# Dealing the half tiles of K and V to the partitions in another order, in a two-layer decode kernel on one core

## The chip, the cores and the metric

The kernel runs on one core of a Trainium2 chip, and the other cores are idle. The metric is the time of one execution on the device, in microseconds (us). The kernel before has three runs, 320.61, 322.80 and 325.11 us; the median is 322.8 us.

## What is computed

One decode step (a single new position) for a batch of four goes through attention, feed-forward, attention and feed-forward again, with the same weights and the same cache both times. Cut to what matters:

```python
B, Sq, D, Hq, Hkv, Sk, Dh, F = 4, 1, 512, 32, 8, 4096, 128, 1792   # all bfloat16

def attention(x):                     # 4 query heads share a K/V head
    q = (x @ wq) by heads
    p = softmax(q @ k_cache.T * Dh ** -0.5)      # over 4096 keys
    return (p @ v_cache) by heads @ wo

def feed_forward(x):
    return (sigmoid(x @ w_gate) * (x @ w_up)) @ w_down

for layer in range(2):
    x = x + attention(layernorm(x))
    x = x + feed_forward(layernorm(x))
```

The K cache and the V cache hold 4 x 8 x 4096 x 128 bfloat16 each, 33.5 MB each. A softmax and the sum over values that follows do not depend on the order of the keys, as long as K and V are in the same order.

## The kernel before

**Units and half tiles.** A unit is one batch row b, one group hg of four K/V heads and one layer l: 4 x 2 x 2 = 16 units, in the order of the list `seq` (L483). A unit has four streams s (one K/V head each), and each stream's 4096 keys are loaded as two half tiles, q = 0 and 1, of K and two of V. A half tile is [128 partitions x 2048 elements], 16 keys of 128 elements in each partition, 512 KB in all. In the kernel before, partition p owns the 32 keys from 32p on: 8 KB of the source. Half tile q takes the 4 KB of them that hold the keys 32p + 16q to 32p + 16q + 15 (L514). So a half tile's source is 128 rows of 4 KB, 8 KB apart, spread over the 1 MB of its stream.

**The ring and the queue.** Half tiles go to a ring of 23 slots (`SLOTS`, L371; `ring`, L384). Every load of K, V and weights is issued by SyncE (SP), one after the other, in the order in which `load_kv` (L509), `load_w` (L520) and the lists of L559 to L581 write them down. Before a load into a slot that was used, SP waits for the instructions that read the slot's last content. Layer 2 reads the cache again. Only the units with hg = 1 of layer 2 find their half tiles still in the ring (`kept`, L492): those of (b, 1, 0) stay in 16 of the slots until (b, 1, 1) has used them, and meanwhile seven slots turn. That makes 96 half tiles of K and 96 of V that are loaded.

**The planner.** The class `_Plan` (L68) takes each operation with a cost, a rank and the names that it reads and writes, plays the program through with an own model of the engines and the DMA (`DMA_RATE` L13, `schedule` L127), and fixes the order on each engine, the slots, and the semaphore waits. A load has size 0.524 and cost 0.5 there (L516). During idle time of TensorE the planner puts filler matmuls (L1119) that compute nothing that is used.

**What happens to a half tile.** A K half tile is transposed in place by VectorE in 32x32 blocks of 4-byte words (L747), then TensorE multiplies it with the queries (L756) into the scores. Scores of both half tiles of a stream are summed into one bank per unit, each half using its own shifted window of the query tile (`window`, L734), so that the probabilities of q = 0 and q = 1 stay in separate rows. The maximum, the exponential and the transposes of the probabilities follow (L778 to L813). A V half tile is multiplied as it lies by the transposed probabilities (L838). After that come the copy out of the bank (L849), the sums over partitions (L854, L861) and the output projection (L870).

**Feed-forward.** For each batch row, `chain` (L984) computes the norm, gate and up products (L932), the gated product (L952 to L964), the down product (L974) and the norm again, from which the queries of layer 2 are made. The last one, for all four rows together, is `last_chain` (L1032) after the last values.

The weights come through the same queue: wq as two loads of 2 MB, wo as four of 1 MB, wg, wu and wd as one load each of 1.75 MB.

Of the kernel before, what the change touches and what calls it, by code (L numbers as in the profile page):

```python
# [348 lines left out]
def bass_interleave_layers__gqa_block_cached__glu_gated_glu__decode_kernel(nc, A_x, A_k, A_v, A_wq, A_wo, B_x, B_wg, B_wu, B_wd, out):  # L349
# [5 lines left out]
    P = 128  # L355
# [4 lines left out]
    NS = 4  # L360
# [4 lines left out]
    TH = T // 2  # L365
# [130 lines left out]
    def tile(kind, b, hg, l, s, q):  # L496
        if l == 1 and hg == 1 and (s, q) in kept[kind]:
            l = 0
        key = (kind, b, hg, l, s, q)
        if key not in tiles:  # L500
            tiles[key] = _Tile(key)
        return tiles[key]

    def fresh(kind, hg, l, s, q):
        return not (l == 1 and hg == 1 and (s, q) in kept[kind])
# [3 lines left out]
    def load_kv(kind, u, s, q):  # L509
        b, hg, l = u  # L510
        if not fresh(kind, hg, l, s, q):
            return
        t = tile(kind, b, hg, l, s, q)
        src = (A_k if kind == "k" else A_v)[b, hg * NS + s].rearrange("(p t) d -> p t d", p=P)[:, q * TH:(q + 1) * TH, :]  # L514
        src = src.rearrange("p t d -> p (t d)")
        S.put("sp", lambda e: e.dma_start(ring[t.slot], src), dma="ring", load=t, size=0.524, cost=0.5)  # L516
        sent[0] += 0.524 / DMA_RATE
        place[kind, u, s, q] = sent[0]
# [25 lines left out]
    def mixed(uk, uv, by):  # L544
        k, v = k_order(uk), v_order(uv)
        for n in range(0, len(k), by):
            for t in k[n:n + by] + v[n:n + by]:
                load_kv(*t)

    def alone(order):  # L550
        for t in order:
            load_kv(*t)
# [607 lines left out]
```

## Time and profile before

| what | value |
| --- | --- |
| runs | 320.61, 322.80, 325.11 us |
| profiled execution: own time | 324.57 us |
| profiled execution: span | 322.9 us |
| mean granted TensorE clock | 0.873 |
| read from HBM | 114.56 MB, 355 GB/s over the span |
| DMA packets | 34931 |
| half tiles of K: issues, median from issue to landing | 96, 9.6 us |
| half tiles of V: issues, median from issue to landing | 96, 14.3 us |
| transposes of K on VectorE (L747) | 96, 1230 ns each, 116.9 us |

The span goes from the first to the last instruction of the profiled execution. Busy times are given as a share of that span. The page also cuts the span into 40 slices of 8.07 us; a digit there is the busy share in tenths, and "GB/s" is what the 16 DMA engines moved in the slice. In the chain that ended last, "DMA" stands for time in which a transfer was on its way, "SPq" for SP's queue.

### The profile page before, as it was taken

How to read it: one execution, taken by the hardware profiler on the slowest of the kernel's cores; microseconds unless marked ns; L12 is line 12 of the kernel's file. 1: busy time of each engine (PE TensorE's matmuls, PEld its weight loads, DVE VectorE, ACT ScalarE, POOL GpSimd, SP SyncE). 2: the span in 40 equal slices, each digit the busy share in tenths (PEclk: the TensorE clock that was granted, in tenths of full speed). 3: DMA queues.
4: the chain of work that ended last, by engine and by line, in shares of the span. 5: the costliest groups of instructions: out<-in, count | busy, mean ns of one | idle time of the engine just before them, and what ended most of it. 6: DMA issues, size and time to landing. Idle time of an engine off the chain costs nothing.

```text
span 322.9 us, 7748 instructions
## 1 busy us (share of the span) xinstructions
PE 216.9 (67%) x3401; PEld 115.8 (36%) x3401; DVE 169.6 (53%) x314; ACT 60.6 (19%) x151; POOL 12.6 (4%) x44
## 2 busy tenths in 40 slices
PE   1243455486869864878774797686896776758685
PEld 1213114333436431335522346233444332324343
DVE  3677250582011889215978326787327777537112
ACT  0202010003102311122131232050322322200301
POOL 8000000000000000000000000000000000000001
PEclk9999995969785987689979999878998999586978
DMA  7999999999999999999799999899998799999910
GB/s 266 402 411 409 401 376 352 404 410 409 396 406 354 306 414 411 407 394 317 229 338 410 410 409 336 287 399 370 412 390 338 202 407 410 409 406 410 393 45 3
DMA packets 34931, 115.09 MB, mean 356 GB/s; under 512 B 3280, under 2 KB 7376, under 8 KB 34896
## 3 DMA queue, kind: packets, MB, share of 16 engines
q1 hardware_dynamic: 34832, 114.57, 93.5%
q8 instruction: 27, 0.44, 0.6%
q14 instruction: 8, 0.07, 0.0%
q10 hardware_dynamic: 64, 0.01, 0.0%
HBM read 114.56 MB, written 0.00 MB: 355 GB/s over the span
## 4 chain that ended last, share of the span: by engine, by line
DMA 54%; PE 21%; SPq 9%; DVE 9%; issue 3%; ACT 2%; POOL 0%; DVEq 0%; ACTq 0%
DMA ring<-in_A_v_cache_dram 24%; DMA ring<-in_A_k_cache_dram 18%; SPq L516 7%; DMA wd<-in_B_w_down_dram 7%; DMA wo<-in_A_wo_dram 6%; DVE ring L747 5%; PE O_ps L838 5%; PE S_ps L756 4%; PE G_ps L974 2%; PE PT_ps L1119 2%; PE M_ps L870 2%; SPq L521 2%; PE Q_ps L676 1%; PE G_ps L932 1%; PE U_ps L932 1%
## 5 line engine op out<-in xcount | busy, mean ns | idle before, releaser
L747 DVE STREAM_TRANSPOSE ring<-ring 128x1024 int32<-128x1024 int32 x96 | 116.9, 1230 | 32.3 <-DMA ring<-in_A_k_cache_dram 31.1
L756 PE MATMUL S_ps<-ring,qz 128*32 128x512 bf16 x512 | 46.0, 485 | 28.6 <-DVE ring L747 26.7
L838 PE MATMUL O_ps<-ring,pt_sb 128*16 128x512 bf16 x512 | 45.8, 443 | 23.5 <-DMA ring<-in_A_v_cache_dram 21.9
L1119 PE MATMUL PT_ps<-even 128*128 128x256 bf16 x311 | 55.1, 317 | 8.1 <-ACT pt_sb L813 3.4
L1119 PEld LDWEIGHTS PT_ps<-even 128*128 128x128 bf16 x311 | 30.9, 114 | 28.3 <-issue 9.9
L849 ACT ACTIVATE b<-O_ps 128x512 bf16<-128x512 f32 x32 | 19.0, 595 | 81.0 <-PE O_ps L838 80.9
L756 PEld LDWEIGHTS S_ps<-ring,qz 128*32 128x32 bf16 x512 | 13.5, 110 | 48.7 <-DVE ring L747 30.5
L792 ACT ACTIVATE pp<-S_ps,tr 128x512 bf16<-128x512 f32 x16 | 13.3, 832 | 73.8 <-DVE tr L785 70.0
L838 PEld LDWEIGHTS O_ps<-ring,pt_sb 128*16 128x16 bf16 x512 | 9.8, 90 | 40.8 <-issue 21.7
L778 DVE TENSOR_REDUCE stat<-S_ps 128x1 f32<-128x512 f32 x16 | 10.9, 684 | 23.1 <-PE S_ps L756 23.1
L861 DVE TENSOR_TENSOR oT<-M_ps,rl 128x8 bf16<-128x8 f32 x32 | 4.8, 149 | 32.4 <-PE M_ps L854 32.3
L870 PE MATMUL M_ps<-oT,wo 128*128 128x32 bf16 x512 | 16.1, 180 | 5.7 <-DMA wo<-in_A_wo_dram 3.4
L870 PEld LDWEIGHTS M_ps<-oT,wo 128*128 128x128 bf16 x512 | 14.4, 98 | 9.6 <-issue 5.4
L854 PE MATMUL M_ps<-sel_o,b 128*128 128x32 bf16 x128 | 8.5, 181 | 9.2 <-ACT b L849 7.0
L922 POOL TENSOR_TENSOR stat<-stat 128x1 f32<-128x1 f32 x8 | 4.3, 543 | 232.1 <-ACT stat L918 232.1
L854 PEld LDWEIGHTS M_ps<-sel_o,b 128*128 128x128 bf16 x128 | 5.5, 98 | 20.1 <-ACT b L849 16.7
L813 ACT ACTIVATE pt_sb<-PT_ps 128x512 bf16<-128x512 f32 x16 | 9.5, 596 | 15.5 <-PE PT_ps L803 15.5
L817 PE MATMUL M_ps<-sel_h,stat 128*128 128x16 f32 x32 | 6.7, 285 | 6.9 <-ACT pp L792 6.6
L882 DVE SCALAR_TENSOR_TENSOR x<-M_ps,x 128x4 f32<-128x4 f32 x16 | 2.5, 156 | 16.0 <-PE M_ps L870 16.0
L974 PE MATMUL G_ps<-pp,wd 128*128 128x32 bf16 x256 | 7.4, 179 | 4.7 <-DVE pp L964 4.7
L798 DVE STREAM_TRANSPOSE pp<-pp 128x256 int32<-128x256 int32 x16 | 6.9, 431 | 6.0 <-ACT pp L792 6.0
L676 PE MATMUL Q_ps<-small,wq 128*128 128x32 bf16 x256 | 8.1, 179 | 2.4 <-issue 2.2
(112 smaller groups left out, 161.6 us busy)
## 6 DMA issues: line engine op xcount, KB each, us to landing
ring<-in_A_k_cache_dram SPq DMA_DIRECT2D x96, 512.0 KB, 9.6
ring<-in_A_v_cache_dram SPq DMA_DIRECT2D x96, 512.0 KB, 14.3
wq<-in_A_wq_dram SPq DMA_DIRECT2D x2, 2048.0 KB, 13.9
wo<-in_A_wo_dram SPq DMA_DIRECT2D x4, 1024.0 KB, 15.1
wg<-in_B_w_gate_dram SPq DMA_DIRECT2D x1, 1792.0 KB, 16.2
wu<-in_B_w_up_dram SPq DMA_DIRECT2D x1, 1792.0 KB, 20.3
wd<-in_B_w_down_dram SPq DMA_DIRECT2D x1, 1792.0 KB, 22.2
xin<-in_A_x_dram ACTq DMA_DIRECT2D x1, 4.0 KB, 3.4
```

The source lines that it names most:

```text
L516: S.put("sp", lambda e: e.dma_start(ring[t.slot], src), dma="ring", load=t, size=0.524, cost=0.5)
L676: fns.append(lambda e, c=c, k=k: e.matmul(Q_ps[:, c * WIDE:(c + 1) * WIDE], lhsT=wq[:, hg, k, c * DH:(c + 1) * DH], rhs=xT[:, b, k:k + 1]. ...
L747: "dve", lambda e, t=t: e.transpose(ring[t.slot].bitcast(dt.int32), ring[t.slot].bitcast(dt.int32)),
L756: fns.append(lambda e, s=s, t=t, nn=nn, q=q: e.matmul(S_ps[qi][32 * s:32 * s + 32, :], lhsT=window(qi, s * NQ + nn, q), rhs=ring[t.slot].r ...
L778: dve(lambda e: e.tensor_reduce(ml[at], bank, AX.X, ALU.max, negate=True), keys(f"S{qi}", ss), keys("ml", ss), 0.7)
L792: lambda e: e.activation(p_sb[at].rearrange("p (t j r) -> p t r j", j=32, r=2), bank.rearrange("p (t r j) -> p t r j", r=2, j=32), ACTF.Ex ...
L838: fns.append(lambda e, m=m, at=at, v=v, c=c, q=q: e.matmul(O_ps[m:m + 16, :], lhsT=pt[:, at:at + 16], rhs=ring[v.slot][:, c * 512:(c + 1) ...
L849: "act", lambda e: e.activation(b1[:], O_ps[:], ACTF.Copy),
L854: fns.append(lambda e, tt=tt: e.matmul(M_ps[:, 0:WIDE], lhsT=b1[:, tt * P:(tt + 1) * P], rhs=sel_o[:, tt, :].unsqueeze(1).broadcast_to([P, ...
L870: fns.append(lambda e, k=k, n=n, h0=h0: e.matmul(M_ps[:, k * WIDE:(k + 1) * WIDE], lhsT=wo[:, h0 + n, k * P:(k + 1) * P], rhs=oT[:, b, h0 ...
L974: fns.append(lambda e, k=k, c=c, rows=rows: e.matmul(o_ps[:, k * WIDE:(k + 1) * WIDE], lhsT=wd[:, c, k * P:(k + 1) * P], rhs=rows.unsqueez ...
L1119: S.filler(lambda e: e.matmul(PT_ps[:, 0:256], lhsT=ident, rhs=flat_even[:, 0:256], start=True, stop=True), "PT")
```

## The change

One source pattern changes, that of the half tiles of K and V. Before, half q of a stream was the q-th 4 KB of every partition's 8 KB. After, half q is the q-th straight 512 KB of the stream, 2048 neighbouring keys. It is seen as 128 runs of 4 KB (16 keys); run number 16i + e, with i from 0 to 7 and e from 0 to 15, goes to partition 8e + i. Two neighbouring runs of the source are thus eight partitions apart. The source pattern has the levels e (16), i (8) and the 4 KB; the destination is the same slot with 128 partitions.

```diff
         t = tile(kind, b, hg, l, s, q)
-        src = (A_k if kind == "k" else A_v)[b, hg * NS + s].rearrange("(p t) d -> p t d", p=P)[:, q * TH:(q + 1) * TH, :]
-        src = src.rearrange("p t d -> p (t d)")
+        src = (A_k if kind == "k" else A_v)[b, hg * NS + s, q * TH * P:(q + 1) * TH * P].rearrange("(i e t) d -> e i (t d)", i=8, e=16)
         S.put("sp", lambda e: e.dma_start(ring[t.slot], src), dma="ring", load=t, size=0.524, cost=0.5)
```

K and V are dealt in the same way, so the key in a given partition and place of a K half tile is the key in that place of the V half tile. Nothing else in the program differs.

## The prediction

> **What bounds the kernel now.** First the page's busy shares and its 40 slices.
>
> ```profile
> PE 216.9 (67%) x3401; PEld 115.8 (36%) x3401; DVE 169.6 (53%) x314; ACT 60.6 (19%) x151; POOL 12.6 (4%) x44
> ...
> DMA  7999999999999999999799999899998799999910
> GB/s 266 402 411 409 401 376 352 404 410 409 396 406 354 306 414 411 407 394 317 229 338 410 410 409 336 287 399 370 412 390 338 202 407 410 409 406 410 393 45 3
> ```
>
> No engine is full, but the transfers are, from the start to slice 37. Many slices stand at 406 to 414 GB/s and none goes beyond: that is a ceiling. Others lie at 200 to 350 although the busy digit stays at 8 or 9. The list of queues and the chain of waits say the same: nearly everything is one queue, and the chain is mostly half tiles on their way.
>
> ```profile
> q1 hardware_dynamic: 34832, 114.57, 93.5%
> ...
> DMA 54%; PE 21%; SPq 9%; DVE 9%; issue 3%; ACT 2%; POOL 0%; DVEq 0%; ACTq 0%
> DMA ring<-in_A_v_cache_dram 24%; DMA ring<-in_A_k_cache_dram 18%; SPq L516 7%; DMA wd<-in_B_w_down_dram 7%; DMA wo<-in_A_wo_dram 6%; DVE ring L747 5%; PE O_ps L838 5%; PE S_ps L756 4%; PE G_ps L974 2%; PE PT_ps L1119 2%; PE M_ps L870 2%; SPq L521 2%; PE Q_ps L676 1%; PE G_ps L932 1%; PE U_ps L932 1%
> ```
>
> Third, stretches by window. The columns are start and end, length, busy time of PE, PEld, DVE, ACT and POOL, the granted clock, DMA share and GB/s.
>
> ```profile
> 161.50:165.00 3.50, 2.32 (x33) 1.00 (x35) 2.55 (x4) 1.27 (x4) 0.00 (x0) 0.66 0.88 247
> 166.00:176.00 10.00, 6.30 (x90) 2.89 (x82) 9.40 (x15) 2.35 (x5) 0.00 (x0) 1.00 1.03 411
> 253.50:257.50 4.00, 3.08 (x54) 1.57 (x58) 3.77 (x6) 1.74 (x5) 0.00 (x0) 1.00 0.84 235
> 260.00:270.00 10.00, 7.82 (x170) 3.86 (x158) 6.71 (x15) 2.76 (x7) 0.00 (x0) 1.00 1.02 412
> 47.00:53.00 6.00, 2.62 (x62) 1.74 (x62) 1.03 (x4) 1.76 (x4) 0.00 (x0) 0.75 1.10 348
> 75.00:80.00 5.00, 3.41 (x75) 1.73 (x63) 0.33 (x2) 1.09 (x2) 0.00 (x0) 1.00 1.03 409
> ```
>
> The reader is to see two states of the same stream. In the even state (166 to 176, 260 to 270) 512 KB come at 411 GB/s: 1.28 us for each half tile. Just after the stream had run dry (161.5 to 165, 253.5 to 257.5) the engines are 84 to 88% busy and move only 235 to 247. The trace's packet records give the mechanism: in the even state a 4 KB packet takes 159 ns at the median, and its eight packets and one 4-byte packet of 9 ns per engine make 8 x 159 + 9 = 1281 ns, the 1.28 us again. After a break the same packets take anything from 159 to some 400 ns for two or three half tiles, and then all fall back to 159. No half tile is missing then, since SP issues one every half microsecond; the engines get in each other's way until they have fallen into step. The half tiles issued at 158.4, 158.7 and 159.4 have their first landing increments at 161.26, 163.30 and 165.29: 2.02 us each. The last two windows are straight weights: 1 KB packets of wo at 348 GB/s, mostly 3.5 KB packets of wg and wu at 409.
>
> Fourth, why the stream runs dry: SP's own waits.
>
> ```profile
> SPq L516 <- PE O_ps L838: 39.6, 16, 8.6
> ...
> SPq L516 <- PE S_ps L756: 22.4, 9, 7.8
> ```
>
> SP waits for readers to give back a slot of the ring. Most of these waits lie under half tiles that are already queued; the rest are the breaks at slices 12, 13, 18, 19, 24, 25, 30 and 31.
>
> **The budget.** The last landing is at 309.45 us. Bytes begin to flow at 2.9 (the first wq lands at 8.0, less 5.1 for its 2 MB). The weights need, by their landings, 2 x 5.1 (wq), 4 x 3.0 (wo), 4.5, 4.5 and 4.65 (wg, wu, wd): 35.9. 192 half tiles x 1.28 are 245.8. That leaves 309.45 - 2.9 - 35.9 - 245.8 = 24.9. Adding up every landing that comes later than its size asks for gives 22.9; the other 2 are the spread of the last half tile over the engines (3.5 us from its first increment to its last). Of the 22.9, 11.8 fall where the half tile had long been issued and others were queued (the slow restarts), 11.1 where it had been issued too late (no free slot). After 309.45 come 13.4 us of last values, projection and feed-forward. Span 322.9; this execution's own time is 324.57, 1.7 more, and the median of the three runs is 322.8, 1.8 less.
>
> **The change part by part.** Removed: a source of 128 rows of 4 KB with a step of 8 KB over 1 MB. Added: a source of 16 x 8 runs of 4 KB in one straight 512 KB; run 16i + e goes to partition 8e + i. Moved: nothing. Cost, size, rank and order given to the planner are the same, so SP's program, the 23 slots, the waits and all compute instructions stay. A half tile now holds other keys, the same for K as for V, and a sum over all keys does not care: 0 us.
>
> Bytes and packets: 4 KB runs before and after, 25,600 such packets: 0. Were they cut to 1 KB, wo's 348 GB/s would make 1.51 us of 1.28, 192 x 0.23 = 44 us; nothing in the pattern asks for it.
>
> SP's issue: a ring issue takes 0.33 to 0.45 us when nothing holds it, and wq, whose destination has one level more, took 0.43. I take 0. Even 0.1 us more is covered by the 1.28 us that a half tile moves; uncovered it would be 192 x 0.1 = 19 us.
>
> The transfer itself: no row shows a source whose outermost count (16) differs from the destination's (128), so which engine gets what is not in the trace. Bounds: at best every half tile takes 1.28 us, as only 133 of the 25,600 packets of 4 KB took under 158 ns and the even state sits at 159 already, and the slow restarts go too: -11.8 us. At worst two engines share one place all the time: 2 x 1.28 = 2.56 us, 192 x 1.28 = +246 us, less the 11.8 that it contains. The nearest row between is the restart, 2.02 us. I take that row: even streaming is an arrangement of 16 engines that needs two or three half tiles to form and is lost at every break, the new source redeals the engines at each half tile, and it can hardly win where the stream is at its floor, while it can lose there 192 times.
>
> [...]
>
> What is late next: with 2.02 us a half tile, the seven slots that still turn while 16 wait for a chain last 14 us where they lasted 9, so the 11.1 us of late slots, the longest pieces of which are 2.8 and 4.0, go to about 0 (kept as upper end: 11). DVE's transposes (1.23 us each, every second half tile) and PE stay beside the stream. PE would idle more; a lower clock in the last 13.4 us (9.4 of them PE) could cost some 4, taken as 0.
>
> Sum: 2.9 + 35.9 + 192 x 2.02 (387.8) + 3.5 spread + 13.4 = 443.5 span, + 1.7 = 445 as against 324.57 of this execution; against the median, 1.8 lower, 443.
>
> **The rivals.** (1) Forecast, engines meet all along: 443. For it: the restarts. Against it: wg and wu, straight and packed, ran at 409. Its own range is 380 (1.69 us each) to 548 (2.56). (2) A small loss: one packet time, 0.16 us, per half tile, 31 us, of which the 11 of late slots absorb a part: 345. (3) Nothing changes: the engines fall into step as before: 323. For it: the floor of 159 ns, and 3.5 KB straight runs at 409; against it: a new deal. (4) Faster: 16 engines read 64 KB side by side and start in step, so the restarts lose their 11.8 us: 322.8 - 11.8 = 311. It decides at the breaks only: if 161.5 to 165 runs at 400 instead of 247. Against it: the first wq, after no traffic at all, was nearly even from its start (368 GB/s from 2.5 to 8), so stepping apart is no certain remedy.
>
> **Chances.** (1) 0.70, (2) 0.06, (3) 0.10, (4) 0.14. A measurement of this kernel can tell about 2% from no change. (1) and (2) are slower: 0.76; (3) the same: 0.10; (4) faster: 0.14. The predicted time is that of (1), 443. The range takes in (2) and (3): from 317, which leaves out most of (4) (0.10), to 540, which leaves out the end of (1) (0.06).
>
> **What would show it.** Even stretches of the changed kernel well under 300 GB/s at DMA share 1.0, with packets over 200 ns, prove the step of 2.02. The chain should show DMA above 70%, SP's waits for slots nearly gone. If the even stretches stand at 410 again, (1) is wrong and the breaks at 145 to 165 and 245 to 258 decide between (3) and (4). A packet count far from 34,931 would refute the step on packets.

## The result, and the profile after

The kernel after takes 444.89 us at the median of four runs (440.23 to 465.87), the kernel before 323.62 at the median of its four. The ratio is 1.362, with a 95% interval of 1.345 to 1.380: the change costs 36%. Two of the four runs after (449.23, which is the profiled one, and 465.87) were over 1.5% above the fastest, and the ratio is taken from the other two, 440.23 and 440.55. The shares and rates below are those of the profiled execution, with a span of 447.5 us.

The same lines of the page as before (busy shares of DMA and GB/s in 40 slices of 11.2 us, the queue, the chain):

```profile
DMA  8999999999999999996999999999999999999960
GB/s 268 257 312 264 264 290 314 264 263 285 375 280 288 281 302 305 292 274 163 237 238 239 241 240 245 246 243 241 241 242 246 251 254 257 257 259 285 295 188 2
DMA packets 34931, 115.09 MB, mean 257 GB/s; under 512 B 3280, under 2 KB 7376, under 8 KB 34896
...
q1 hardware_dynamic: 34832, 114.57, 97.5%
...
DMA 75%; PE 11%; SPq 7%; DVE 4%; issue 2%; ACT 1%; POOL 0%; DVEq 0%; ACTq 0%
```

The DMA engines are as busy as before, and the count of packets is the same to the last one; but the ceiling of 410 GB/s is gone, and most slices stand at 240 to 310. The chain is three quarters transfers. By window (start, end, length, busy time of PE, PEld, DVE, ACT and POOL, granted clock, DMA share, GB/s):

```profile
170.00:180.00 10.00, 6.04 (x59) 2.03 (x60) 1.48 (x7) 0.60 (x1) 0.00 (x0) 0.53 1.03 306
224.00:250.00 26.00, 13.33 (x152) 6.33 (x152) 10.80 (x22) 3.43 (x7) 0.00 (x0) 0.61 1.03 239
410.00:430.00 20.00, 12.28 (x104) 4.56 (x102) 5.81 (x11) 2.56 (x5) 0.00 (x0) 0.67 1.03 296
```

At a DMA share of 1.03, as in the even state of before, 239 to 306 GB/s come instead of 411. The 4 KB packets, 159 ns then, are 289 ns at the median from 224 to 250 us and 228 from 410 to 430; a half tile lands 2.03 us after the one before it at the median. The rate has a history: it stands at 303 from 161 to 176 us, is lowest right after the break at slice 18 (landings every 2.2 us from 216 us on), and climbs to 295 at the end (1.7 us). The pattern of a transfer is the same all the time, so the loss depends on something that lasts from one half tile to the next. How the engines stand to each other in time is the reading taken here; no record shows the place of a single engine.

### The profile page after: what moved, and what is told of

Same layout as the page of the kernel before. It is cut to its first block, busy times and chain, and to the rows that moved or that the text cites. A ratio compares the mean times of both kernels' runs of the same rounds, so it can differ in the third digit from the quotient of the medians.

```text
span 447.5 us, 7748 instructions
## 1 busy us (share of the span) xinstructions
PE 252.2 (56%) x3401; PEld 124.2 (28%) x3401; DVE 172.3 (38%) x314; ACT 60.6 (14%) x151; POOL 12.6 (3%) x44
## 2 busy tenths in 40 slices
DMA packets 34931, 115.09 MB, mean 257 GB/s; under 512 B 3280, under 2 KB 7376, under 8 KB 34896
## 4 chain that ended last, share of the span: by engine, by line
DMA 75%; PE 11%; SPq 7%; DVE 4%; issue 2%; ACT 1%; POOL 0%; DVEq 0%; ACTq 0%
DMA ring<-in_A_v_cache_dram 37%; DMA ring<-in_A_k_cache_dram 32%; SPq L515 6%; DMA wo<-in_A_wo_dram 6%; PE O_ps L837 4%; PE S_ps L755 3%; DVE ring L746 2%; PE PT_ps L1118 1%; PE M_ps L869 1%; SPq L520 1%; PE G_ps L931 1%; ACT b L848 0%; PE U_ps L931 0%; ACT pp L791 0%; PE M_ps L853 0%
## 5 line engine op out<-in xcount | busy, mean ns | idle before, releaser
L746 DVE STREAM_TRANSPOSE ring<-ring 128x1024 int32<-128x1024 int32 x96 | 118.9, 1240 | 99.7 <-DMA ring<-in_A_k_cache_dram 99.5
L837 PE MATMUL O_ps<-ring,pt_sb 128*16 128x512 bf16 x512 | 57.0, 533 | 78.0 <-DMA ring<-in_A_v_cache_dram 76.7
L755 PE MATMUL S_ps<-ring,qz 128*32 128x512 bf16 x512 | 53.6, 556 | 59.4 <-DVE ring L746 53.4
L1118 PE MATMUL PT_ps<-even 128*128 128x256 bf16 x311 | 63.4, 351 | 7.6 <-ACT pt_sb L812 2.9
L1118 PEld LDWEIGHTS PT_ps<-even 128*128 128x128 bf16 x311 | 33.4, 122 | 33.6 <-issue 12.4
L755 PEld LDWEIGHTS S_ps<-ring,qz 128*32 128x32 bf16 x512 | 14.4, 120 | 82.6 <-DVE ring L746 57.3
L869 PEld LDWEIGHTS M_ps<-oT,wo 128*128 128x128 bf16 x512 | 15.0, 102 | 14.3 <-DVE oT L860 7.7
L719 ACT ACTIVATE maskrs<-mask,stat 128x16 f32<-128x16 f32 x16 | 4.8, 304 | 37.4 <-DVE qz L724 29.1
L816 PEld LDWEIGHTS M_ps<-sel_h,stat 128*128 128x128 f32 x32 | 6.3, 246 | 12.5 <-ACT pp L791 9.7
## 6 DMA issues: line engine op xcount, KB each, us to landing
ring<-in_A_k_cache_dram SPq DMA_DIRECT2D x96, 512.0 KB, 13.4
```

The lines of the kernel that those rows point to most:

```text
L746: "dve", lambda e, t=t: e.transpose(ring[t.slot].bitcast(dt.int32), ring[t.slot].bitcast(dt.int32)),
L755: fns.append(lambda e, s=s, t=t, nn=nn, q=q: e.matmul(S_ps[qi][32 * s:32 * s + 32, :], lhsT=window(qi, s * NQ + nn, q), rhs=ring[t.slot].r ...
L816: "pe", lambda e: e.matmul(M_ps[:, hs], lhsT=ls[at].broadcast_to([len(ss) * 32, P]), rhs=sel_h[at, hs], start=True, stop=True,),
L837: fns.append(lambda e, m=m, at=at, v=v, c=c, q=q: e.matmul(O_ps[m:m + 16, :], lhsT=pt[:, at:at + 16], rhs=ring[v.slot][:, c * 512:(c + 1) ...
L869: fns.append(lambda e, k=k, n=n, h0=h0: e.matmul(M_ps[:, k * WIDE:(k + 1) * WIDE], lhsT=wo[:, h0 + n, k * P:(k + 1) * P], rhs=oT[:, b, h0 ...
L1118: S.filler(lambda e: e.matmul(PT_ps[:, 0:256], lhsT=ident, rhs=flat_even[:, 0:256], start=True, stop=True), "PT")
```

## The experiments

The theory at first: the 16 x 8 source makes each engine write eight neighbouring partitions, and engines then meet at their destinations. This is the author's estimate: no record shows which engine writes which partitions. The rival: reading a straight 512 KB with 16 engines close together is what is slow. The diffs show only the part of the source pattern that changes; e2 and e4 start from the kernel before, the others from the kernel after. "Outer count" is the number of steps of the source's outermost level, and an "index" is one of these steps.

**e1: Undo the deal, keep the straight block.**

```diff
-"(i e t) d -> e i (t d)", i=8, e=16
+"(p t) d -> p (t d)", p=P
```

> The straight 512 KB of the change, but run p goes to partition p, so source and destination both count 128 outermost. The theory of the deal (engines meet because the 16 x 8 source makes each engine write eight neighbouring partitions) expects the even state of before: half tiles at 1.28 us, 4 KB packets at 159 ns, 318 to 328 us in all. The rival theory of the addresses (reading one straight 512 KB with 16 engines close together is what is slow) expects it to stay slow: over 400 us, packets over 230 ns. A gain of up to 10 us on before would say that straight reading mends the restarts.

Measured: 315.07 us (313.43 to 316.44) against 323.26, ratio 0.976 (0.969 to 0.984). Windows of its profile, the first of them right after the break at 155 us:

```profile
158.40:162.00 3.60, 2.59 (x38) 1.18 (x42) 3.35 (x5) 0.97 (x4) 0.00 (x0) 0.63 1.03 422
160.00:180.00 20.00, 14.84 (x209) 6.62 (x209) 14.06 (x26) 4.81 (x10) 0.00 (x0) 0.85 1.03 411
```

The straight block is no harm; it helps: the interval lies wholly below 1, at a gain of 1.6 to 3.1%. After the break the half tiles' first landings come at 158.25, 159.53, 160.81 and 162.09, 1.28 us apart at once, where the kernel before had 2.02. So reading a straight 512 KB is not what makes the loss.

**e2: Keep the deal, undo the straight block.**

```diff
-src = src.rearrange("p t d -> p (t d)")
+src = src.rearrange("(i e) t d -> e i (t d)", i=8)
```

> The 128 rows of before, 8 KB apart over 1 MB, but dealt like the change: row 16i + e to partition 8e + i. The theory of the deal expects the time of the change, 430 to 460 us, with 4 KB packets of some 250 ns. The theory of the addresses expects about 323 us, since the straight 512 KB is undone.

Measured: 457.27 us, ratio 1.420 (1.405 to 1.434). The deal alone costs all of it, and without the straight block it costs a little more than the change does (ratio 1.420 against 1.362).

**e3: A 16 x 8 source without the step of eight.**

```diff
+.rearrange("(e h i t) d -> e h i (t d)", e=16, h=2, i=8)[:, q]
```

> A source of 16 x 8 in which neighbouring runs stay on neighbouring partitions: half q takes eight neighbouring 4 KB runs out of each group of sixteen, so each engine would read 32 KB straight and engines are 64 KB apart, and nothing is dealt with a step. The theory of the deal expects the time of the change, 430 to 460 us, because only the count 16 matters. The theory of the addresses, and one in which the step of eight between neighbouring runs is to blame, expect 318 to 328 us.

Measured: 450.05 us, ratio 1.397 (1.379 to 1.415). Here neighbouring runs do go to neighbouring partitions. The slices of the two kernels, e2 and then e3, look like those of the change:

```profile
GB/s 265 239 304 250 252 256 328 252 254 268 395 250 271 278 281 280 280 282 233 131 240 240 238 240 240 244 242 252 253 258 263 257 255 255 255 265 281 283 162 2
```

```profile
GB/s 260 253 302 248 249 253 331 256 261 261 397 259 266 262 262 261 262 270 294 149 244 251 254 257 258 255 243 245 248 251 253 255 255 253 258 268 286 296 213 2
```

Slice 10 in both is the weights, dealt by 128, at 395 and 397: on the same queue, in the same execution, they run at nearly the full rate. Three address patterns with an outer count of 16 are slow alike (ratios 1.36 to 1.42), so neither the addresses nor the order of keys is the main cause.

**e4: Old addresses, old keys, but two transfers to 64 partitions each.**

```diff
-lambda e: e.dma_start(ring[t.slot], src)
+[lambda e, n=n: e.dma_start(ring[t.slot][n:n + 64], src[n:n + 64]) for n in (0, 64)]
```

A slot now gets two transfers, so whoever waits for it counts 32 increments of its semaphore where it counted 16.

> Before's addresses and order of keys, but each half tile goes as two transfers, to partitions 0 to 63 and 64 to 127. [...] If only the 16 against 128 were to blame, for instance through the cost of walking the source, it stays at 323 to 335 us (twice the transfers to issue, 0.43 us each, are still below 1.28 us).

Measured: 469.73 us (465.55 and 473.90). The window 270 to 330 of its profile:

```profile
270.00:330.00 60.00, 34.40 (x548) 17.94 (x544) 28.10 (x49) 9.98 (x26) 1.08 (x2) 0.76 1.04 245
```

Source and destination are dealt alike here, and every byte comes from where it came from before. Each transfer still has its 16 small packets (6352 packets under 512 B in all, 3280 before: 16 more for each half tile). What has changed is that a transfer writes 64 partitions and not 128, and the rate falls to 245 GB/s at full DMA share (1.04), with 4 KB packets of 269 ns at the median of the whole run. So no difference of counts between source and destination is needed for this loss. Two other things changed as well: other rows are read at one time, and a transfer has 256 KB instead of 512. The rows are an unlikely cause, since with 4, 8, 12 and 16 KB between them (e1, before, e10, e5) a half tile takes the same 1.28 us; transfers of 256 KB to all 128 partitions were not tried. (SP's issues doubled too: its share of the chain is 26%, against 7% in the change. But at a DMA share of 1.04 the engines were not waiting for it.)

**e5: Is it the distance of the reads that mends the restarts?** Half tiles from two heads, runs 16 KB apart.

```diff
+.rearrange("h (p c t) d -> (h p) c (t d)", c=4, t=16)[:, s % 2 * 2 + q]
```

> Plain deal to 128 partitions, but the 4 KB runs of a half tile lie 16 KB apart over the 2 MB of two neighbouring heads (before 8 KB, in the straight kernel 4 KB), so half tiles hold keys of two heads and the output is not the reference's. If the slow restarts come from the distance at which the engines read, they get worse than before: restarts of over 2.0 us a half tile, 323 to 340 us, with an even state still at 1.28 us. If the distance does not matter and only the straight block does, 320 to 326 us as before.

Measured: 319.87 us, ratio 0.997 (0.992 to 1.002): no difference. Restarts stay uneven, but not worse than with 8 KB:

```profile
158.00:161.50 3.50, 1.50 (x25) 0.85 (x29) 2.76 (x8) 1.67 (x4) 0.00 (x0) 0.98 1.00 277
```

The distance as such is not it.

**e6: Only K dealt.**

> K half tiles dealt as in the change, V half tiles as before; K and V are then in different orders, so the output is not the reference's. If the cost belongs to each dealt half tile, 96 of 192 pay 0.75 us: half of the change's 120 us, 375 to 395 us, K landings at about 2.0 us and V landings at 1.28. If one dealt stretch leaves the engines out of step for the plain one behind it, V is slow too and the time comes out over 410 us.

Measured: 402.38 and 409.63 us, more than the sum by half tiles and less than the other theory asked. Between two half tiles of one kind (85 intervals each) K lands 2.17 us apart on average (1.52 before, breaks included) and V 1.36 (1.29 before). Over all 96 intervals that end with a K half tile the rise is 66 us, 0.69 each, and over the 96 that end with V it is 12; together they are the 78 us by which the last landing is later. Most of the cost does belong to the dealt half tile, and a part spills into the plain ones behind it: the first V half tile after K comes at 1.85 us on average, where it was 1.30.

**e7: An outer count of 8.**

```diff
-"(i e t) d -> e i (t d)", i=8, e=16
+"(i e t) d -> e i (t d)", i=16, e=8
```

> The straight 512 KB seen as 8 x 16 runs: run 8i + e to partition 16e + i. If the deal goes along the outermost count of the source, only eight engines can take part: DMA share about 0.5 and at best 2.55 us a half tile, 192 x 1.27 = 244 us more than the straight kernel, 560 us or more; more still (up to 5.1 us) where two of the eight meet. If the deal goes by the destination's 128, it is like the change, 430 to 460 us.

Measured: 574.29 us, in one run. The page's slices of 14.3 us:

```profile
DMA  6855677579655555555355555555555555555540
GB/s 225 218 209 209 221 247 247 209 222 227 228 208 211 211 210 210 210 208 208 100 129 130 182 211 211 212 210 208 210 208 212 210 211 211 210 209 209 211 200 4
```

Half the DMA share and 210 GB/s, half of 410: eight engines take part, each at full rate. The semaphores say the same: a slot's semaphore gets one update some 0.4 us after SP's instruction and eight as the half tile lands, where the change has sixteen; and the page counts 33395 packets where the change has 34931, eight fewer for each of the 192 half tiles. After the break at slice 19 they move 129 and 130 at the same share, and the 4 KB packets there (286 to 315 us) are 252 ns at the median and 321 at the 99th percentile, about twice 159. That fits engines that meet in pairs. Two slices later they are at 211, with packets of 159 ns again.

**e8: An outer count of 64.**

```diff
-"(i e t) d -> e i (t d)", i=8, e=16
+"(i e t) d -> e i (t d)", i=2, e=64
```

> The straight 512 KB seen as 64 x 2 runs: run 64i + e to partition 2e + i. The deal along the source gives each of 16 engines four of the 64, which are eight neighbouring partitions as in the change: 430 to 460 us. If a count of 64 were enough for the deal of 128 rows, 313 to 326 us.

Measured: 314.72 us, in one run. The expectation of a loss fell: counts that differ are no harm by themselves. If eight neighbouring partitions to an engine are what is slow, the engines cannot have got four neighbouring indices each here. A new theory came from it: the even state can be had as long as one index of the outer count does not span too many partitions. Two are fast here (1.28 us a half tile at the median) and eight are slow (2.03); that four are still fast was the author's estimate.

**e9: An outer count of 32, four partitions to an index.**

```diff
-"(i e t) d -> e i (t d)", i=8, e=16
+"(i e t) d -> e i (t d)", i=4, e=32
```

> The straight 512 KB seen as 32 x 4 runs: run 32i + e to partition 4e + i, so one index of the source's outermost count covers four partitions instead of eight. The theory that the good deal gives each engine groups of four partitions, and can be had as long as no index of the outermost count spans more than four, expects the fast time: even state 1.28 us, 312 to 318 us. If the deal changes as soon as the counts of source and destination differ by more than two, it is slow like the change, 430 to 460 us.

Measured: 316.15 us, ratio 0.985 (0.979 to 0.990), with the even state:

```profile
160.00:180.00 20.00, 13.94 (x198) 6.38 (x190) 13.19 (x25) 4.74 (x9) 0.00 (x0) 0.83 1.02 407
```

Four partitions to an index are fast (1.28 us a half tile) and eight are slow (2.03), with the same bytes, packets and issues; whether an engine writes groups of four was not shown. With 128 partitions, though, "eight partitions to an index" and "an outer count of 16" are one and the same; no run separates them.

**e10: Runs 12 KB apart.**

```diff
+r0 = (0, 1, 2, 384, 385, 386, 640, 641)[n]
...
+[b, hg * NS:(hg + 1) * NS].rearrange("h (r t) d -> (h r) (t d)", t=16)[r0:r0 + 382:3]
```

Here n = 2s + q counts the eight half tiles of a unit.

> Plain deal to 128 partitions, 4 KB runs 12 KB apart over 1.5 MB; a half tile mixes heads and some keys are read twice and others not at all, so the output is not the reference's. The straight kernel (4 KB apart) restarts evenly, those with 8 and 16 KB do not. If it takes an uninterrupted block to restart evenly, this one is like before, 318 to 325 us with restarts of about 2 us a half tile. If only even multiples of 4 KB are bad, because all runs of a half tile then agree in an address bit, it restarts like the straight kernel, 312 to 317 us.

Measured: 313.36 us, ratio 0.974 (0.969 to 0.980), with even restarts: 419 GB/s from 157.8 to 161.4, just after its break:

```profile
157.80:161.40 3.60, 2.63 (x56) 1.23 (x60) 3.60 (x5) 1.19 (x2) 0.00 (x0) 1.00 1.03 419
```

So it takes no uninterrupted block. Steps of 4 and 12 KB restart evenly; 8 and 16 KB do not.

**e11: The outer count of 64, timed.**

> The straight 512 KB as 64 x 2 runs again, timed against before: 312 to 318 us, the same as the straight kernel with 128 rows within one per cent, as both have the even state at 1.28 us and even restarts. If dealing neighbouring runs to different engines helps beyond the straight block, it is under 312.

Measured: 314.42 us, ratio 0.978 (0.970 to 0.986), the same as the straight kernel with 128 rows within their intervals. This deal brings nothing beyond the straight block. Of the kernels that compute the reference these two have the lowest ratios (0.976 and 0.978; the interval of e9, 0.985, overlaps theirs), and the straight one with 128 rows is the simplest.

## Why the prediction was right, point by point

**The bound and the even state.** Right. No run's half tiles came faster than 8 x 159 + 9 ns at the median: e1, e5, e8, e9, e10 and e11 all have a median interval of 1.28 us.

**The transfer, 2.02 us a half tile.** Right in size: 2.03 us at the median, and all 192 together, breaks included, took 390.5 us where the sum had 387.8. The weights took 37.9 where it had 35.9, and the spread of the last half tile 2.7 where it had 3.5. That engines get in each other's way fits packets over 200 ns at full DMA share, the history after a break, and e4; the meeting itself was not seen. Two of the reasons given for it failed. The loss does not come because source and destination count differently: 64 x 2 and 32 x 4 differ as well, are new sources too, and keep the even state. What goes with the loss in transfers to 128 partitions is an outer count of 16, where an index spans eight partitions. And the restart, from which the 2.02 was taken, is another effect: it goes away when the rows of the plain deal are 4 or 12 KB apart (e1, e10), while the change reads a straight block and is slow all the same, and e2 is slow with the rows of before. So the agreement of 2.02 with 2.03 is luck; within the one profile the interval went from 1.7 to 2.2 us. The sign set out, stretches well under 300 GB/s, came after the break at slice 18 (239 from 224 to 250 us), but from 161 to 176 us it was 303.

**The worst case, 2.56 us a half tile.** That two engines share one place all the time was the author's estimate, worked out as 2 x 1.28; no run shows such a place, or which engine wrote which partitions. Measured were 2.03 us at the median and 2.2 in the slowest stretch. What the runs show is a border: 1.28 us in e9, with four partitions to an index, and 2.03 in the change, with eight. In e4, with 64 partitions to a transfer, 245 GB/s were measured; its two halves follow each other in the queue, and whether they overlapped in time was not seen.

**Packets and bytes, 0.** Right: 34931 before and after.

**SP's issue, 0 (at most 0.1 us more).** The size was off: an issue takes 0.60 us at the median where 0.43 was the row, 0.17 more, also in e9, which is fast. So it was hidden, as the step said, below 1.28 us.

**What is late next.** Half right. The late slots did not go to 0. Call a half tile issued late if 2.6 us after its issue (about the shortest time from issue to first landing, 2.66 us, in the kernel before) is past the moment when an even stream would land it. Then 9 us of the 22.9 before are late issues and 14 slow restarts. The split depends on that limit: with 3.0 us it is 11.6 and 11.3, near the prediction's 11.1 and 11.8. By the same rule (2.6 us) some 7 us are late issues after the change, most of it at the break at slice 18, where two landings are 6.6 us apart. And "SP's waits for slots nearly gone" was wrong, they grew:

```profile
SPq L515 <- PE O_ps L837: 46.4, 16, 11.2
...
SPq L515 <- PE S_ps L755: 29.4, 6, 9.6
```

39.6 and 22.4 us before. SP runs ahead of the queue and waits for slots that slower half tiles fill later; most of such a wait is no loss of its own, since only those 7 us of landings were late for it.

**The tail.** 447.5 - 434.0 (last landing) = 13.5 us, as in the sum (13.4). The lower clock that the prediction weighed did not come: from 434 to 447.5 us the granted clock was 0.87, where the same stretch had 0.75 before.

**The rivals.** "A small loss" and "nothing changes" did not happen. The faster one was a true effect under the loss: without the deal, the straight block takes off 8.2 us (323.26 - 315.07) of the 11.8 that it could. By the count above the slow restarts are 14 us before, 10 in e5, 3 in e1 and 2 in e10; but in e1 the late issues rise from 9 to 13 us, so a part of that gain is lost again, as it would be if a faster stream runs into the slots sooner. Against e1, the deal is a loss of some 130 us (444.89 - 315.07), and the straight block a gain of some 8. The two do not simply add: with the deal in place (e2) the straight block is worth 457.27 - 444.89 = 12.4 us.

## What to carry to other kernels

Before changing the shape of a load, ask how its outermost count deals it out. Here, with 4 KB runs to 128 partitions, a count of 8 kept half of the engines idle (DMA share 0.51), 16 cost some 40% (444.89 us against 315.07), and 32, 64 and 128 were as good as each other (316.15, 314.42 and 315.07). Keep it at 128, or time the new count against 128. Check the time of a packet at full DMA share, since a busy digit of 9 stood here beside 411 GB/s (before) and beside 239 (after) alike. If a straight block and a new deal come in one edit, time them apart: here the one was worth 2.4% and the other cost 40%.

## What the runs showed of the hardware that was not expected

With the plain deal to 128 partitions, the restart after a dry queue depends on the step of the runs: with 8 KB (before) and 16 KB, two or three half tiles come some 2 us apart, with 4 and 12 KB they come at 1.28 us, nearly from the first. The dealt 64 x 2 of the straight block lies between: after its break at 152 us one interval is 1.62 us (e11). In the first two all runs of a half tile agree in the address bit that counts 4 KB, in the others they do not. This fits the four runs; the place in memory at which the engines would meet was not seen, and no step other than these four was tried.

With the deal of 16 the engines don't fall into an even state after a break as they do with 128: 200 us were not enough (239 GB/s from 224 us on, 296 at 420). With the eight engines of e7 some 40 us were. Why they differ is open.
